# Masked global rows transposed by the DMA crossbar instead of TensorE, with mask tables for odd batches and a band mask from ScalarE

## Chip, cores and metric

One core of a Trainium2 chip. The metric is the device time of one execution in microseconds (us). Each execution is marked as fast or slow by its clock and span.

## The reference, cut to what matters

Attention over 8 batches, 8 heads, 576 positions and head size 64, followed by a gated feed-forward block on the 4608 tokens that result (model width 512, inner width 1536). A position sees its neighbours within 32 places; 8 global positions see everything and are seen by all.

```python
def _attn_ref(q, k, v, global_idx):
    ...
    mask = np.abs(pos[:, None] - pos[None, :]) <= 32
    mask = mask | is_global[:, None] | is_global[None, :]
    scores = np.where(mask, scale * (q @ k.T), -1e9)
    ...                                   # softmax, then times v

def _moe_ref(x, w_gate, w_val, w_out):
    g = x @ w_gate
    silu = g * (1.0 / (1.0 + np.exp(-g)))
    return silu * (x @ w_val) @ w_out
```

## The kernel before

The kernel splits each batch's attention into a band part and a global part. For the global part it gathers the 8 global rows of k and q, places them in a masked block `kqm` (128 partitions x 2 x 128, bf16), and transposes that to `gT`. `step_S2` multiplies `gT` with all keys, `step_SG` with all queries.

```python
def gather_mask(b, kg, qg, eng=None):
    kqms[b] = gw.tile([P, 2, 2, D], BF16, tag="kqm", name="kqm", bufs=4)
    for a, src in ((0, kg), (1, qg)):
        (eng or nc.gpsimd).tensor_tensor(
            out=kqms[b][:, a], in0=bc(src, [[0, 2], [1, D]]),
            in1=bc(mka[:, (a + b) % 2, :], [[1, 2], [0, D]]), op=ALU.mult)
...
def step_GT():
    kqm = kqms[b]
    ps = mtile([P, 2, P], BF16, "ps_g")
    for a in range(2):
        nc.tensor.transpose(out=ps[:, a, :],
            in_=kqm[:, a].rearrange("p r d -> p (r d)"), identity=ident)
    st["gT"] = gw.tile([P, 2, P], BF16, tag="gT", name="gT")
    if b % 2 == 0:
        nc.vector.tensor_copy(out=st["gT"], in_=ps)
        return
    cols = "p t (h a x) -> p (t h) a x"           # odd batches: halves swapped by the copy
    dst, src = (t.rearrange(cols, h=HP, a=2) for t in (st["gT"], ps))
    for a in range(2):
        nc.vector.tensor_copy(out=dst[:, :, a], in_=src[:, :, 1 - a])
```

The feed-forward block runs as 9 chunks of 512 tokens with 16 units each. The attention of batch b is put between the units of the chunk before its own: a table says after which unit each step goes. What SyncE and GpSimd issue (casts of k and q to bf16, crossbar transposes, loads) is placed by unit too. The code calls the point after a unit a gap. The texts below use that word, and call a unit of gate and value matmuls a gate. A casting copy (cast for short) is a DMA that turns float32 into bf16 on its way, and a DMA's landing is the moment at which it reports that it is done.

```python
        if b == 2:
            return {
                1: [L(step_GT), vb],
                2: [L(step_S2), L(step_SG)],
                ...
        return {
            1: [L(step_GT), vb],
            2: [L(step_S2), L(step_SG)] + ([L(step_P2T)] if b >= XP else []),
            ...
    cast_at, tr_at, v_at, g_at, m_at = {3: 13, 4: 26}, {2: 11, 3: 21}, {2: 8}, {2: 6}, {2: 12}
    ...
        if b > 4:
            cast_at[b] = o - 32 + 8               # o = 16 * (b - 1)
        ...
            if b % 2 == 0:
                m_at[b] = o - 16 + 13             # kqm of batches b and b + 1
```

A unit is eight gate and value matmuls or twelve output matmuls, 2.3 us on average. So the transposes come one unit before they are used. The table orders what is on one engine; GpSimd does not wait for TensorE's units, only for its own inputs and buffers (79.5 us in all until TensorE was done with a `va` buffer), and so issues the casts of k and q for batch b + 2 about when batch b's global rows are due: those of batch 6 at 142.06 and 143.76, where batch 4's rows are used at 148.52. In the head, GpSimd issues the loads of batch 1 after clearing some buffers:

```python
    def loads_b():
        kT_clear(1, nc.gpsimd)
        va_clear(1, nc.gpsimd)
        gather_mask(1, *g0)
        loaded[1] = new_qk()
        load_qk_part(1, loaded[1], 0)             # k and q of batch 1
        ...
```

The softmax here doesn't subtract the row's maximum and nothing guards it: scores larger than these inputs give would overflow.

## Time and profile before

| | before |
|---|---|
| median of 4 runs (lowest to highest) | 358.79 us (358.1 to 360.75) |
| span of the profiled run, mean clock | 356.9 us, 1.000 |
| TensorE busy | 345.9 us, 97% |
| TensorE's longest wait on a DMA after the head | none listed |
| time of one chunk in the quiet part (chunks 4 to 7) | 37.09 to 37.10 us |

The span runs from the first to the last instruction. "Busy" leaves out waits, so 97% on TensorE says that nearly all the time is TensorE's own work. The last row is my own reading of the timeline: the times at which ScalarE finishes copying the last output block of a chunk, one subtracted from the next. I use these chunk ends throughout, as they say *where* in the span a change gains or loses. The prediction below shows the profile's lines.

### The profile page before, as it was taken

To read this page: it belongs to the slowest core of one execution; us is meant where nothing else is said; L and a number is where in the kernel's file an instruction comes from. 1 tells how busy PE (TensorE), PEld (TensorE's weight loads), DVE (VectorE), ACT (ScalarE), POOL (GpSimd) and SP (SyncE) were. 2 spreads that over 40 slices of the span, in tenths; PEclk is the share of its full clock that TensorE was granted. 3 is DMA by queue.
4 is the path that set the end of the run, shared out by engine and by line. 5 is a ranking of instruction groups with operands and counts; after the bars stand their busy time and mean duration, and the time that the engine had idled before them with its cause. 6 is when DMAs were issued, how large, how long until landed. Compare 5 with 4: busy or idle time off the path is not lost.

```text
span 356.9 us, 7667 instructions
## 1 busy us (share of the span) xinstructions
PE 345.9 (97%) x3105; PEld 167.9 (47%) x3155; DVE 231.8 (65%) x469; ACT 152.9 (43%) x236; POOL 91.9 (26%) x110
## 2 busy tenths in 40 slices
PE   7889999999999999999999999999999999999996
PEld 2455445444544444444444444444444444444444
DVE  5777785289818883689368935885488637715750
ACT  4775663464324542454244522553255323323322
POOL 7974664805235113401291011000000000000000
PEclk9999999999999999999999999999999999999999
DMA  7999999999999997995899979723330230011002
GB/s 104 148 204 204 184 212 159 160 251 157 155 165 234 157 124 140 161 207 80 135 169 155 147 119 156 117 49 77 111 78 2 61 96 32 0 59 62 0 20 99
DMA packets 153540, 44.14 MB, mean 124 GB/s; under 512 B 140065, under 2 KB 148001, under 8 KB 153505
## 3 DMA queue, kind: packets, MB, share of 16 engines
q0 software_dynamic: 101216, 19.14, 65.1%
q1 hardware_dynamic: 52288, 24.51, 32.8%
q8 instruction: 24, 0.39, 0.5%
q14 instruction: 12, 0.09, 0.1%
HBM read 38.02 MB, written 16.52 MB: 153 GB/s over the span
## 4 chain that ended last, share of the span: by engine, by line
PE 90%; DVE 3%; POOL 2%; ACT 2%; issue 2%; POOLq 0%; DVEq 0%
PE pg L791 26%; PE po L852 25%; PE pv L791 25%; PE ps_s L510 3%; PE ps_av L597 3%; POOL va L102 1%; PE ps_av L588 1%; PE ps_s L444 1%; PE po L839 1%; PE ps_av L479 1%; PE ps_t L387 1%; PE ps_av L624 1%; PE pg L809 1%; PE ps_av L616 1%; PE pgv L791 0%
## 5 line engine op out<-in xcount | busy, mean ns | idle before, releaser
L791 PE MATMUL pg<-xT,wg_sb 128*128 128x512 bf16 x398 | 106.5, 380 | 1.6 <-issue 0.2
L791 PE MATMUL pv<-xT,wv_sb 128*128 128x512 bf16 x413 | 106.6, 379 | 0.2
L824 DVE SCALAR_TENSOR_TENSOR gv<-th,pg 128x512 bf16<-128x512 bf16 x107 | 73.3, 686 | 50.3 <-ACT th L822 49.5
L822 ACT ACTIVATE th<-pg 128x512 bf16<-128x512 f32 x107 | 63.9, 598 | 80.4 <-PE pg L791 78.8
L852 PE MATMUL po<-wo_sb,h 128*128 128x512 bf16 x400 | 92.7, 380 | 0.8
L828 DVE TENSOR_TENSOR h<-gv,pv 128x512 bf16<-128x512 bf16 x107 | 73.6, 688 | 11.5 <-PE pg L791 0.5
L791 PEld LDWEIGHTS <-wv_sb 128*128 128x128 bf16 x424 | 41.5, 98 | 50.0
L852 PEld LDWEIGHTS <-h 128*128 128x128 bf16 x420 | 39.4, 98 | 45.4
L791 PEld LDWEIGHTS <-wg_sb 128*128 128x128 bf16 x424 | 38.4, 98 | 43.8 <-issue 2.1
L102 POOL DMA_DIRECT2D va<-in_v_dram x40 | 35.1, 970 | 90.2 <-PE ps_av L597 79.5
L857 ACT ACTIVATE osb<-po 128x512 f32<-128x512 f32 x35 | 20.9, 597 | 81.7 <-PE po L852 67.0
L543 ACT ACTIVATE pe<-ps_s 128x1024 bf16<-128x1024 f32 (+1 forms) x39 | 36.4, 936 | 17.9 <-PE ps_s L510 17.8
L549 DVE TENSOR_TENSOR pt<-pe,band 128x1024 bf16<-128x1024 bf16 (+1 forms) x39 | 24.8, 635 | 15.3 <-ACT pe L543 14.4
L570 DVE TENSOR_TENSOR xa<-ps_av,den 128x512 bf16<-128x512 f32 (+1 forms) x40 | 25.5, 638 | 1.4
L564 DVE TENSOR_REDUCE den<-ps_av 128x8 f32<-128x16 f32 (+1 forms) x40 | 6.7, 167 | 27.5 <-PE ps_av L597 25.2
L510 PEld LDWEIGHTS <-kT 64*128 64x128 bf16 x576 | 10.7, 95 | 15.4 <-issue 15.1
L109 POOL DMA_DIRECT2D kf<-in_k_dram x6 | 13.4, 2236 | 15.9 <-issue 10.2
L109 POOL DMA_DIRECT2D qf<-in_q_dram x6 | 16.0, 2661 | 1.5 <-DMA qf<-in_q_dram 1.5
L510 PE MATMUL ps_s<-qT,kT 64*128 64x64 bf16 x576 | 15.4, 191 | 0.1
L597 PE MATMUL ps_av<-va,pt 128*64 128x66 bf16 x256 | 14.3, 197 | 0.0
L597 PE MATMUL ps_av<-vb,pt 128*64 128x66 bf16 x256 | 14.2, 197 | 0.0
L597 PEld LDWEIGHTS <-pt 128*64 128x64 bf16 x512 | 10.8, 110 | 4.2
(140 smaller groups left out, 199.9 us busy)
## 6 DMA issues: line engine op xcount, KB each, us to landing
out_dram<-osb SPq DMA_DIRECT2D x35, 256.0 KB, 2.2
vb<-va SPq DMA_DIRECT2D x14, 264.0 KB, 5.3
kf<-in_k_dram POOLq DMA_DIRECT2D x6, 576.0 KB, 16.8
qf<-in_q_dram POOLq DMA_DIRECT2D x6, 576.0 KB, 18.7
va<-in_v_dram POOLq DMA_DIRECT2D x24, 128.0 KB, 11.7
va<-in_v_dram POOLq DMA_DIRECT2D x16, 96.0 KB, 7.7
wg_sb<-in_moe_w_gate_dram POOLq DMA_DIRECT2D x3, 512.0 KB, 10.1
wv_sb<-in_moe_w_val_dram POOLq DMA_DIRECT2D x3, 512.0 KB, 12.0
```

The source lines that it names most:

```text
L102: nc.gpsimd.dma_start(out=va[lo:hi, u, :, 0:D], in_=vs[t0 + lo : t0 + hi])
L109: nc.gpsimd.dma_start(out=t, in_=src[b].rearrange("h s d -> s h d"))
L510: nc.tensor.matmul(out=ps[:, par, 64 * slot : 64 * slot + 64], lhsT=kT[r : r + 64, hp, 64 * t : 64 * t + P], rhs=qTs[b][r : r + 64, hp, 64 ...
L543: nc.scalar.activation(out=pe, in_=ps[:, :, 0 : 64 * ns].rearrange("p r (s c) -> p r s c", c=64), func=AF.Exp, scale=SCALE,)
L549: mult = lambda: nc.vector.tensor_tensor(out=pt.rearrange("p r s c -> p (r s) c"), in0=pe.rearrange("p r s c -> p (r s) c"), in1=bc(band, ...
L570: nc.vector.tensor_tensor(out=xa.rearrange("p (g h) d -> p g h d", g=g), in0=bc(ps, pst + [[1, D]]), in1=bc(den, [[4, g], [1, 4], [0, D]]) ...
L597: nc.tensor.matmul(out=ps[64 * e : 64 * e + 64, hg, hl, :], lhsT=pt[:, hl % 2, 4 * (hl // 2) + 2 * (tp % 2) + e, :], rhs=(va if e == 0 els ...
L791: nc.tensor.matmul(out=ps[:, 0:n], lhsT=w[:, cc, P * fc : P * (fc + 1)], rhs=xT[:, cc, t0 : t0 + n], start=(cc == 0), stop=(cc == NCC - 1),)
L822: nc.scalar.activation(out=th[:, 0:n], in_=pg[:, 0:n], func=AF.Tanh, scale=0.5)
L824: nc.vector.scalar_tensor_tensor(out=gv[:, 0:n], in0=th[:, 0:n], scalar=1.0, in1=pg[:, 0:n], op0=ALU.add, op1=ALU.mult,)
L828: nc.vector.tensor_tensor(out=st["h"][:, fc, 0:n], in0=gv[:, 0:n], in1=pv[:, 0:n], op=ALU.mult)
L852: nc.tensor.matmul(out=po, lhsT=st["h"][:, fc, P * ts : P * (ts + 1)], rhs=wo_sb[:, fc, :], start=(fc == 0), stop=(fc == NFC - 1),)
```

## The change

Its intent is to take work off the engine that bounds the kernel. For batches 2 to 7 the two TensorE transposes and VectorE's copy of `gT` give way to one crossbar transpose by DMA, issued by SyncE. One transpose of the whole block does not swap halves as VectorE's copy did for odd batches, so these get mask tables of their own, made by GpSimd in the head. The transposed probabilities of batch 3 go to the crossbar as well (`XP`). And the band mask, which GpSimd used to make, now comes from a square on ScalarE and a compare on VectorE, with one of the `vb` copies (`shift` 3) moved from ScalarE to GpSimd.

```diff
+    XG = 2
-    XP = 4
+    XP = 3
...
-    band = const.tile([P, 64], BF16)          # GpSimd: memset and two affine_selects
...
     def loads_b():
+        tables_odd()
...
     def squares():
+        nc.scalar.activation(out=bsq, in_=iq[:, 0:64], func=AF.Square, bias=pcol, scale=1.0)
...
     def tables_a():
+        nc.vector.tensor_scalar(out=band, in0=bsq, scalar1=R2, scalar2=None, op0=ALU.is_lt)
...
+        nc.scalar.copy(out=cnt.rearrange("p (i c) -> p i c", i=2), in_=ps_i[:, :, 0:320])
+
+    def tables_odd():
+        nc.gpsimd.memset(mg[:, 0:WIN], 0.0)
+        nc.gpsimd.memset(mg[:, WIN + S : KC], 0.0)
+        nc.gpsimd.tensor_scalar(
+            out=mg2o, in0=cnt, scalar1=thi[:, 1:2], scalar2=None, op0=ALU.is_lt
+        )
+        nc.gpsimd.tensor_tensor(out=mg2o, in0=mg2o, in1=mg, op=ALU.mult)
...
         def step_GT():
             kqm = kqms[b]
+            if b >= XG:
+                st["gT"] = gw.tile([P, 2, P], BF16, tag="gT", name="gT")
+                nc.sync.dma_start_transpose(
+                    out=st["gT"], in_=kqm.rearrange("p a r d -> p (a r d)")
+                )
+                return
...
-            if b % 2 == 0:                    # and the swapping copies of odd batches
-                nc.vector.tensor_copy(out=st["gT"], in_=ps)
-                return
...
-in0=pe, in1=mg, op=ALU.mult)
+in0=pe, in1=(mt if b % 2 else mg)[:, WIN : WIN + S], op=ALU.mult)
...
-in0=pe, in1=mg2, op=ALU.mult)
+in0=pe, in1=mg2o if b % 2 else mg2, op=ALU.mult)
...
-                L(shift, 1, act), L(step_S, 3), ...
+                L(step_S, 3), L(shift, 1, act), L(shift, 3, nc.gpsimd.tensor_copy), ...
...
         if b == 2:
-                1: [L(step_GT), vb],
+                0: [L(step_GT)],
+                1: [vb],
...                                            # b >= 3
-            1: [L(step_GT), vb],
+            -1: [L(step_GT)],
+            1: [vb],
```

The last hunk: the crossbar transpose is issued one or two units earlier than TensorE's transposes were.

More of the change, by code (lines that the diff above doesn't have):

```diff
@@ L159 @@
                    allow_small_or_imprecise_dtypes=True)
+    pcol = const.tile([P, 1], FP32)
+    nc.gpsimd.iota(pcol, pattern=[[0, 1]], base=2 * WIN, channel_multiplier=-1,
+                   allow_small_or_imprecise_dtypes=True)
     load_0("k", 1)
@@ L238 @@
     )
-    thi = const.tile([P, 1], FP32)
+    thi = const.tile([P, 2], FP32)
     nc.vector.tensor_scalar(
-        out=thi, in0=asel[:, 0:1], scalar1=1e6, scalar2=0.5, op0=ALU.mult, op1=ALU.add
+        out=thi, in0=asel, scalar1=1e6, scalar2=0.5, op0=ALU.mult, op1=ALU.add
     )
@@ L279 @@
     load_v(0)
-    band = const.tile([P, 64], BF16)
-    nc.gpsimd.memset(band, 1.0)
-    nc.gpsimd.affine_select(
-        out=band, in_=band, compare_op=ALU.is_ge, fill=0.0,
-        base=0, pattern=[[-1, 64]], channel_multiplier=1,
-    )
-    nc.gpsimd.affine_select(
-        out=band, in_=band, compare_op=ALU.is_ge, fill=0.0,
-        base=2 * WIN, pattern=[[1, 64]], channel_multiplier=-1,
-    )
     load_wgv(0)
@@ L307, in loads_b @@
             )
-    mg = const.tile([P, S], BF16)
+    mg = const.tile([P, KC], BF16)
     mg2 = const.tile([P, KC], BF16)
+    mg2o = const.tile([P, KC], BF16)
+    cnt = const.tile([P, KC], BF16)
     m1 = const.tile([P, KC], BF16)
+    band = const.tile([P, 64], BF16)
+    bsq = const.tile([P, 64], FP32)
     def squares():
+        nc.scalar.activation(out=bsq, in_=iq[:, 0:64], func=AF.Square, bias=pcol, scale=1.0)
         nc.scalar.activation(out=iq, in_=iq, func=AF.Square, bias=ngcol, scale=1.0)
@@ L326, in tables_a @@
         nc.vector.tensor_scalar(
-            out=mg, in0=iq[:, WIN : WIN + S], scalar1=sgn[:, 0:1], scalar2=thr[:, 0:1],
+            out=mg[:, WIN : WIN + S], in0=iq[:, WIN : WIN + S], scalar1=sgn[:, 0:1], scalar2=thr[:, 0:1],
             op0=ALU.mult, op1=ALU.is_gt,
@@ L338, in tables_b @@
         nc.vector.scalar_tensor_tensor(
-            out=mg2.rearrange("p (i c) -> p i c", i=2), in0=ps_i[:, :, 0:320], scalar=thi,
+            out=mg2.rearrange("p (i c) -> p i c", i=2), in0=ps_i[:, :, 0:320], scalar=thi[:, 0:1],
             in1=mt.rearrange("p (i c) -> p i c", i=2), op0=ALU.is_lt, op1=ALU.mult,
         )
+        nc.scalar.copy(out=cnt.rearrange("p (i c) -> p i c", i=2), in_=ps_i[:, :, 0:320])
[6 more added lines that the diff above has]
+        nc.gpsimd.tensor_tensor(out=mg2o, in0=mg2o, in1=mg, op=ALU.mult)
     def warm(*widths):
@@ L409, in step_GT @@
             st["gT"] = gw.tile([P, 2, P], BF16, tag="gT", name="gT")
-            if b % 2 == 0:
-                nc.vector.tensor_copy(out=st["gT"], in_=ps)
-                return
-            cols = "p t (h a x) -> p (t h) a x"
-            dst, src = (t.rearrange(cols, h=HP, a=2) for t in (st["gT"], ps))
-            for a in range(2):
-                nc.vector.tensor_copy(out=dst[:, :, a], in_=src[:, :, 1 - a])
+            nc.vector.tensor_copy(out=st["gT"], in_=ps)
         def step_SG():
@@ L433, in step_SG @@
             st["pg"] = bp.tile([P, S], BF16, tag="pg", name="pg")
-            mult = lambda: nc.vector.tensor_tensor(out=st["pg"], in0=pe, in1=mg, op=ALU.mult)
+            mult = lambda: nc.vector.tensor_tensor(out=st["pg"], in0=pe, in1=(mt if b % 2 else mg)[:, WIN : WIN + S], op=ALU.mult)
             if b == 0:
@@ L455, in step_S2 @@
             st["p2"] = work.tile([P, KC], BF16, tag="p2", name="p2")
-            mult = lambda: nc.vector.tensor_tensor(out=st["p2"], in0=pe, in1=mg2, op=ALU.mult)
+            mult = lambda: nc.vector.tensor_tensor(out=st["p2"], in0=pe, in1=mg2o if b % 2 else mg2, op=ALU.mult)
             if b == 0:
@@ L719, in attention @@
                 L(step_S, 1), L(step_P2T), M("e*"), M("p*", 1), L(shift, 0, dve),
-                L(shift, 1, act), L(step_S, 3), L(warm, 512, 512), L(step_AV2), M("p*", 5),
+                L(step_S, 3), L(shift, 1, act), L(shift, 3, nc.gpsimd.tensor_copy), L(warm, 512, 512), L(step_AV2), M("p*", 5),
                 L(shift, 2, act), L(warm, 512, 512, 512),
                 L(step_AV, 0), M("xa*", 0), L(warm, 512, 256), L(step_AV, 1), M("p*", 3),
-                L(step_X, 0), L(shift, 3, act), L(warm, 256), L(step_AV, 2), M("xa*", 1),
+                L(step_X, 0), L(warm, 256), L(step_AV, 2), M("xa*", 1),
                 L(warm, 512, 512), M("xa*", 2), L(step_X, 1), L(step_AV, 3), M("xa*", 3),
```

## The prediction

No term of its main sum is among them: 4.2 + 1.5 + 3.5 = 9.2 us lost and 0.6 gained, net 8.6, and with it 368 us. GpSimd's new work in the head was put at about 4 us, which gives the 23.5 at which batch 1's loads would be issued. The clock (rival 2) was to bring the time up to 371 us. In the "quiet stretch" at 182.3 a cast had been issued too, 0.5 us before the store (181.78); at 145.3 the two casts had been issued 3.2 and 1.5 us before.

> **What bounds the kernel now.** I read the page first, then the list of waits, then the timeline around one batch's global rows, then the DMA issues of narrow stretches.
>
> From the page:
>
> ```profile
> PE 345.9 (97%) x3105; PEld 167.9 (47%) x3155; DVE 231.8 (65%) x469; ACT 152.9 (43%) x236; POOL 91.9 (26%) x110
> PEclk9999999999999999999999999999999999999999
> DMA  7999999999999997995899979723330230011002
> PE 90%; DVE 3%; POOL 2%; ACT 2%; issue 2%; POOLq 0%; DVEq 0%
> ```
>
> TensorE bounds it: 97% busy, 90% of the chain that ended last, full clock. Four 512-column matmuls take 0.86 us in the chain, 0.216 us each. [...]a microsecond of waiting anywhere after the head is a microsecond at the end. The DMA row matters next: the engines are nearly full for the first 60% of the span (batches 0 to 4) and lightly loaded after that. No wait of TensorE on a DMA stands in the list of waits after the first loads. From the list (engine, line, releaser: total us, times, longest):
>
> ```profile
> DVE pt L549 <- ACT pe L543: 14.4, 26, 3.1
> PEld L444 <- DVE gT L411: 2.4, 4, 1.2
> PEld L444 <- DVE gT L416: 1.3, 3, 0.4
> PE ps_s L444 <- DVE gT L411: 1.0, 1, 1.0
> DVE pt L549 <- POOL band L286: 0.9, 1, 0.9
> ```
>
> L444 is the first use of gT, the transposed global rows. It waits for VectorE's copy, but most of that is weight-load time that overlaps matmuls: the matmuls themselves waited 1.0 us once, for batch 0. The last line is the band mask that GpSimd makes late in the head.
>
> The timeline of batch 4, around its global rows (start, duration):
>
> ```profile
> 145.27 0.53 SPq L859 DMA_DIRECT2D out_dram<-osb  x1
> 145.72 1.03 PE L791 MATMUL pv<-xT,wv_sb 128*128 128x512 bf16 x4
> 146.07 0.47 SPq L129 DMA_DIRECT2D vb<-va  x1
> 146.58 0.28 PE L405 MATMUL ps_g<-ident,kqm 128*128 128x128 bf16 x2
> 146.70 1.03 PE L791 MATMUL pg<-xT,wg_sb 128*128 128x512 bf16 x4
> 147.56 1.03 PE L791 MATMUL pv<-xT,wv_sb 128*128 128x512 bf16 x4
> 148.52 0.46 PE L444 MATMUL ps_s<-kT,gT 128*32 128x320 bf16 x8
> ```
>
> The two transposes cost 146.70 - 146.58 = 0.12 us of TensorE. The rows are needed at 148.52. The built program shows where the crossbar transpose goes in SyncE's queue: behind the output store issued at 145.27 and ahead of the vb copy issued at 146.07. So its neighbours tell when it could land. The DMA issues of the stretches 145.2 to 145.3 and 146.0 to 146.1 (last number: median us to landing):
>
> ```profile
> out_dram<-osb SPq DMA_DIRECT2D x1, 256.0 KB, 6.1
> vb<-va SPq DMA_DIRECT2D x1, 264.0 KB, 7.8
> ```
>
> The store lands at 145.27 + 6.1 = 151.4 and vb at 153.9, both well after 148.52. This reading decides the prediction.
>
> [...]SyncE's transfers land in issue order, 2.2 us after issue for a store in a quiet stretch (182.3) but 6.1 us at 145.3, while GpSimd's casting copies run.[...] The change leaves three gates, about 5 us.[...]
>
> **The change, part by part.**
>
> Removed from TensorE: two transposes in each of batches 2 to 7, 6 x 0.11 = 0.7 us; the gap of about 0.1 us ahead of L444 where VectorE's copy is late, up to 0.5 us; the five transposes of batch 3's masked probabilities, now also on the crossbar, 0.29 us (115.68 to 115.97). Together 1.3 to 1.5 us. VectorE loses about 2.3 us of copies (six of 0.216 and three of 0.284 for batches 2 to 7, and a little in batch 1) and ScalarE a copy of 0.69 us. Both have slack, so nothing comes of it.
>
> Head: the band mask no longer comes from GpSimd (0.74 us of work, and VectorE's wait of 0.94 us until 13.51). The new square of 64 columns on ScalarE (estimate 0.26 us, between 0.20 us for one column and 0.83 us for 640) fits in its 3.0 us wait for ngcol; VectorE's compare fits in its 0.38 us wait before mt. The count copy (estimate 0.70 us, as p2e of the same width) delays exponentials whose results waited for the band anyway. So batch 0's gT copy can start about 0.8 us earlier and the head shortens by up to 0.8 us.
>
> [...]The loads of batch 1, issued at 19.3, would be issued at about 23.5. The weight loads before them keep the engines full until about 28 (GpSimd waits for the last wv_sb until 27.97), so they should land as before, at 29 to 34.
>
> Added on the critical path: waits for gT. Six crossbar transposes must land within 3 to 5 us of being issued.
> - Batch 2: SyncE issues four stores from 67.65, after it was held by the kT and qT transposes. The stores take a median of 7.1 us, the last is issued at 69.3 and lands near 78.0 (its trace landing is 8.7 us after issue). gT comes behind it, near 78.0; L444 began at 73.77. Loss 4.2 us. This time is set by the DMA engines, so the head's gain is swallowed here.
> - Batch 3: stores of that stretch take 6.3 us, the third is issued at 106.58, hence gT near 112.7 against 111.14. Loss 1.5 us.
> - Batch 4: gT near 152.0 against 148.52. Loss 3.5 us.
> - Batches 5 to 7: quiet DMA; crossbar transposes of similar size land in 2.3 to 2.4 us. Issued at about 183.0, 220.1 and 257.6, gT lands at 185.4, 222.5, 260.0 against 185.61, 222.71, 259.80: even, or 0.2 us gained or lost each.
>
> Sum: 4.2 + 1.5 + 3.5 = 9.2 us lost; about 0.6 us gained (0.3 for batch 3's transposes, 0.3 in batches 5 to 7). Net +8.6, or 368 us.
>
> **The rivals.**
> 1. *gT lands in time everywhere.* kqm is ready long before (about 61 us for batches 2 and 3), and a transpose of 64 KB is small. Then the sum is -0.8 (head) - 1.4 = about 357.2 us. For it: the kernel before is scheduled closely and never waits for a DMA (batch 4's p2t, 8.1 us to landing, arrives just in time), so someone may have placed this with care too. Against it[...]landings of 6 to 9 us on both sides of it.
> 2. *The waits cost the clock too.* [...]up to 371 us.
> 3. *The head gets worse.* If GpSimd's new work takes 7 us rather than 4, the loads of batch 1 start late, the engines idle, and batch 1's first transposes (32.6, with about 1.7 us of slack) wait: 1 to 2 us more, which passes on through batch 2's casts. For it: GpSimd's spans stretch[...] (a 128x128 multiply took 0.39 us, but up to 2.0 us once). Against it: some 4 us of queue ahead.
> 4. *The waits shrink each other.* A wait in batch 2 lets the DMA engines catch up, so batches 3 and 4 wait less: about 362 to 364 us. Against it: GpSimd's casts are released by TensorE's progress there, so they shift too.
>
> **Range and chances.** I give the late landing (368, or 362 to 371 with rivals 2 to 4) about 65%, the timely one (357) about 35%. The middle of that mixture is about 366 us. Slower by over 2% means above 366.6, which most but not all of the first case reaches: 0.45. Faster by over 2% would need 352.3, for which no part of the sum is large enough: 0.02. Range 357 to 371.5.
>
> **What would show each step.** Right: new waits of TensorE at ps_s<-kT,gT on the DMA gT<-kqm, 4 us in batch 2, 1 to 2 in batch 3, 3 to 4 in batch 4 and next to nothing in batches 5 to 7, with gT 5 to 9 us from issue to landing in the first three and 2.4 in the rest; a unit of 16 steps in the quiet part (37.09 us, 217.32 to 254.41) shorter by 0.1 to 0.2 us; VectorE's wait on band gone. Wrong: no such waits, gT landing within 4 us under load, and a time near 357; or a wait of batch 1's transposes on k_bf or q_bf, which would be rival 3; or a PEclk digit below 9, rival 2.

## The result, and the profile after

| | before | after |
|---|---|---|
| median of 4 runs (lowest to highest) | 358.79 us (358.1 to 360.75) | 381.46 us (380.26 to 383.14) |
| span and mean clock of the profiled run | 356.9 us, 1.000 | 379.4 us, 0.978 |

The ratio is 1.0626 with a 95% interval of 1.0564 to 1.0687: slower. (Ratios are the mean time of one kernel's fast runs over the mean of the other's fast runs of the same rounds, so not quite the ratio of the medians quoted.) The output was correct. 381.46 us is outside the predicted range of 357 to 371.5.

From the page of the kernel after (busy us and share of the span; then the clock and DMA rows of the 40 slices; then the chain that ended last):

```profile
PE 349.1 (92%) x3088; PEld 168.0 (44%) x3138; DVE 230.3 (61%) x460; ACT 152.0 (40%) x235; POOL 96.2 (25%) x114
...
PEclk9999999969999999969998999999999999999999
DMA  8999999999999938995499959880350051002002
...
PE 59%; DMA 16%; POOL 11%; issue 9%; SPq 2%; DVE 2%; ACT 0%; POOLq 0%
```

TensorE has fewer instructions than before (3088 against 3105) and yet is busy for 3.2 us longer, because three stretches, in slices 9, 18 and 22, ran at a lower clock. The chain that was 90% TensorE is now 59%, with DMA at 16%. TensorE's waits on DMAs after the head, which the kernel before did not have (line and releaser: total us, times, longest):

```profile
PE ps_s L457 <- DMA gT<-kqm: 18.6, 5, 6.8
...
PE ps_av L610 <- DMA vb<-va: 1.4, 1, 1.4
```

L457 is the first use of `gT` (L444 before). Batch by batch, in TensorE's timeline of the kernel after (start, duration, and in brackets how long TensorE had stood and for what):

```profile
79.45 0.72 PE L457 MATMUL ps_s<-kT,gT 128*32 128x320 bf16 x8 [5.92 <-DMA gT<-kqm]
...
121.20 0.46 PE L457 MATMUL ps_s<-kT,gT 128*32 128x320 bf16 x8 [2.87 <-DMA gT<-kqm]
...
205.61 0.72 PE L457 MATMUL ps_s<-kT,gT 128*32 128x320 bf16 x8 [2.09 <-DMA gT<-kqm]
...
282.19 0.46 PE L457 MATMUL ps_s<-kT,gT 128*32 128x320 bf16 x8 [0.94 <-DMA gT<-kqm]
```

Batches 2, 3, 5 and 7; batch 6 did not wait. After two of these the eight matmuls took 0.72 us where they take 0.46 otherwise. Batch 4 with what SyncE did before it, from the timeline of the kernel after:

```profile
156.58 0.33 SPq L874 DMA_DIRECT2D out_dram<-osb  x1
157.02 1.93 SPq L418 DMA_TRANSPOSE gT<-kqm  x1
...
157.22 1.03 PE L806 MATMUL pv<-xT,wv_sb 128*128 128x512 bf16 x4
...
165.04 0.72 PE L457 MATMUL ps_s<-kT,gT 128*32 128x320 bf16 x8 [6.79 <-DMA gT<-kqm]
```

TensorE was through with its last value matmul at 157.22 + 1.03 = 158.25 and had nothing to do until 165.04. Its `gT` had been asked for only 1.2 us before 158.25. From there to the landing it took, in the DMA issues of a narrow stretch of the kernel after around batch 4's (last number: us to landing):

```profile
gT<-kqm SPq DMA_TRANSPOSE x1, 8.0
```

The same view gives 7.8, 6.9, 8.0, 4.7, 2.3 and 2.3 us for batches 2 to 7. The transfer is the same 64 KB each time.

**The clock.** The view of chosen windows of the kernel after (start and end; length, then the busy time of TensorE with its count of instructions, weight loads, VectorE, ScalarE, GpSimd; then granted clock, DMA share and GB/s). In this trace the clock was at half speed from 75.88 to 82.70, from 161.20 to 168.03 and from 205.58 to 208.99, so for 6.82, 6.83 and 3.41 us, and at full speed in between. The windows have the length of the shortest of these; the last two end and begin where the clock fell, and the first two, where it did not, begin 12 and 13 such lengths after 75.88:

```profile
116.84:120.25 3.41, 1.49 (x7) 0.49 (x5) 2.31 (x4) 0.60 (x1) 0.00 (x0) 1.00 1.99 200
120.25:123.66 3.41, 2.41 (x24) 1.22 (x26) 1.07 (x3) 1.80 (x3) 0.00 (x0) 1.00 1.70 231
...
202.17:205.58 3.41, 1.34 (x7) 0.39 (x4) 2.17 (x4) 0.60 (x1) 3.41 (x5) 1.00 1.19 91
...
205.58:208.99 3.41, 3.38 (x22) 1.32 (x23) 0.95 (x2) 1.57 (x3) 0.24 (x1) 0.51 1.92 248
```

At batch 5 TensorE was busy for 1.34 us of one window and the next ran at 0.51, with 3.38 us of matmul time in it. At batch 3 it was busy for 1.49 us and the next ran at full clock. The two stretches at batches 2 and 4, 75.88 to 82.70 and 161.20 to 168.03, have 3.25 and 2.99 us of matmul time in them. At half speed the next four matmuls of 512 columns began after 1.68 us (166.18 to 167.86), at full speed after 0.87 (168.83 to 169.70). So if half of the busy time at half speed is lost, the loss is an estimated 1.6, 1.5 and 1.7 us for batches 2, 4 and 5, together 4.8 us.

**The sum.** How far the kernel after trails the kernel before at the end of each chunk, and what the rows above make of it (us; a batch's wait falls in the chunk of the same number, counted from 1; each transposed batch saves 0.12, batch 3's crossbar probabilities 0.28, and both savings come from the kernels below):

| chunk | behind at its end | added in it | wait | clock | savings | worked out |
|---|---|---|---|---|---|---|
| 1 | -0.19 | -0.19 | | | | |
| 2 | 7.23 | 7.42 | 5.92 | 1.62 | -0.12 | 7.42 |
| 3 | 9.78 | 2.55 | 2.87 | | -0.40 | 2.47 |
| 4 | 17.95 | 8.17 | 6.79 | 1.50 | -0.12 | 8.17 |
| 5 | 21.60 | 3.65 | 2.09 | 1.69 | -0.12 | 3.66 |
| 6 | 21.50 | -0.10 | 0 | | -0.12 | -0.12 |
| 7 | 22.39 | 0.89 | 0.94 | | -0.12 | 0.82 |
| 8 and 9 | 22.40 | 0.01 | | | | |

The profile accounts for the loss: 18.6 us of waits, 4.8 us of clock, 1.0 us saved, against a difference of the spans of 22.5. What is left to test is why `gT` was late, whether the waits alone explain it, and what the rest of the change is worth.

**The head.** GpSimd's timeline, before:

```profile
19.29 0.76 POOL L80 DMA_DIRECT2D k_bf<-in_k_dram  x1
```

and after:

```profile
18.39 2.11 POOL L351 TENSOR_SCALAR mg2o<-cnt,thi 128x640 bf16<-128x640 bf16 x1
20.59 1.61 POOL L354 TENSOR_TENSOR mg2o<-mg2o,mg 128x640 bf16<-128x640 bf16 x1
...
24.87 0.78 POOL L81 DMA_DIRECT2D k_bf<-in_k_dram  x1
```

The new compare and multiply took 3.7 us, and the first load of batch 1 was issued 5.6 us later. By the end of chunk 1 the kernel after is nevertheless 0.19 us ahead. This profiled run had an early head: batch 1's first use of `gT` began 0.90 us sooner than before (41.63 against 42.53), and the wait of 1.4 us on `vb` used that up. The other changed kernels came to that point within 0.4 us of the kernel before.

### The profile page after: what moved, and what is told of

It is laid out like the page before. It is cut to its first block, busy times and chain, and to the rows that moved or that the text cites. A ratio compares the mean times of both kernels' runs of the same rounds, so it can differ in the third digit from the quotient of the medians.

```text
span 379.4 us, 7641 instructions
## 1 busy us (share of the span) xinstructions
PE 349.1 (92%) x3088; PEld 168.0 (44%) x3138; DVE 230.3 (61%) x460; ACT 152.0 (40%) x235; POOL 96.2 (25%) x114
## 4 chain that ended last, share of the span: by engine, by line
PE 59%; DMA 16%; POOL 11%; issue 9%; SPq 2%; DVE 2%; ACT 0%; POOLq 0%
PE pg L806 18%; PE po L867 17%; PE pv L806 17%; DMA gT<-kqm 6%; DMA va<-in_v_dram 5%; POOL va L103 3%; DMA wv_sb<-in_moe_w_val_dram 3%; PE ps_s L523 2%; PE ps_av L610 2%; DMA kg<-in_k_dram,gofs 2%; POOL qf L110 2%; SPq L689 1%; POOL kf L110 1%; PE ps_av L601 1%; PE ps_s L457 1%
## 5 line engine op out<-in xcount | busy, mean ns | idle before, releaser
L806 PE MATMUL pg<-xT,wg_sb 128*128 128x512 bf16 x394 | 109.0, 387 | 1.6
L806 PE MATMUL pv<-xT,wv_sb 128*128 128x512 bf16 x417 | 107.9, 381 | 0.1
L457 PE MATMUL ps_s<-kT,gT 128*32 128x320 bf16 x64 | 4.5, 363 | 18.6 <-DMA gT<-kqm 18.6
L464 ACT ACTIVATE p2e<-ps_s 128x640 bf16<-128x640 f32 x8 | 5.6, 704 | 24.5 <-PE ps_s L457 24.5
## 6 DMA issues: line engine op xcount, KB each, us to landing
kf<-in_k_dram POOLq DMA_DIRECT2D x6, 576.0 KB, 13.8
va<-in_v_dram POOLq DMA_DIRECT2D x24, 128.0 KB, 7.5
```

Source lines behind the costliest of these rows:

```text
L806: nc.tensor.matmul(out=ps[:, 0:n], lhsT=w[:, cc, P * fc : P * (fc + 1)], rhs=xT[:, cc, t0 : t0 + n], start=(cc == 0), stop=(cc == NCC - 1),)
```

## The experiments

The theory: `gT` is asked for too late for a loaded DMA system, TensorE stands, and the stand costs clock as well. The rivals: the new tables and late loads in the head cause the loss; or the wait alone costs and the clock follows from something else; or the output store ahead of it in SyncE's queue is what delays `gT`.

All kernels gave correct output. Medians of 4 runs unless noted; the kernel before ran beside them at 359.02 to 359.05.

| kernel | median us (lowest to highest) | ratio to before, 95% | clock of the profiled run |
|---|---|---|---|
| e1_gt_on_pe | 359.8 (359.32 to 360.68) | 1.0019, 0.9995 to 1.0043 | 0.999 |
| e2_early | 360.23 (359.56 to 360.33) | 1.0022, 1.0003 to 1.0041 | 1.000 |
| e3_fill | 377.25 (377.04 to 379.38) | 1.0519, 1.0482 to 1.0556 | 1.000 |
| e4_head | 381.91 (378.73 to 384.81), one run marked slow | 1.0659, 1.0599 to 1.0718 | 0.982 |
| e5_early_head | 360.88 (360.46 to 361.36) | 1.0051, 1.003 to 1.0071 | 1.000 |
| e6_cast_later | 380.48 (378.94 to 381.27) | 1.0578, 1.0549 to 1.0607 | 0.973 |
| e7_before_store | 374.4 (370.17 to 375.2) | 1.0383, 1.032 to 1.0447 | 0.982 |
| e8_xg3_early_head | 359.19 (358.96 to 360.36), 6 runs | 1.0007, 0.9989 to 1.0025 | 1.000 |

### e1_gt_on_pe: the change without the crossbar rows

```diff
-    XG = 2
+    XG = 8
-                0: [L(step_GT)],
-                1: [vb],
+                1: [L(step_GT), vb],
...
-            -1: [L(step_GT)],
-            1: [vb],
+            1: [L(step_GT), vb],
```

> The changed kernel with the global rows of batches 2 to 7 transposed by TensorE again, at their old places; the odd tables, the band, the shift on GpSimd and batch 3's crossbar p2t stay. Theory (the lost time is the late gT and the clock that falls after it): the five waits on gT, 18.6 us, and the halved clock, about 4.9 us, both go; 357 to 359.5 us. Rival (the rest of the change, head or odd tables, costs several us of its own): 362 us or more.

Measured: 359.8 us, ratio 1.0019, 0.3 us over the range expected. All but about 0.7 us of the loss is in the crossbar rows; tables, band mask, moved copy and batch 3's probabilities together leave the time the same within noise. TensorE's list of waits of this kernel has no `gT` from a DMA but has a new one in batch 2:

```profile
PE ps_sg L435 <- DMA qT<-qf: 1.0, 1, 1.0
```

It is ahead of the kernel before by 0.23 us at the end of chunk 1, behind by 0.95 at the end of chunk 2, and by 0.67 to 0.73 from chunk 3 on. So the later loads of the head cost about 1 us in batch 2, where the queries come late (in e8, with the loads early again, that wait is 0.32 us), and batch 3's probabilities on the crossbar give back 0.28.

### e2_early: the crossbar rows issued five units earlier

```diff
-                0: [L(step_GT)],
+                -5: [L(step_GT)],
...
-            -1: [L(step_GT)],
+            -6: [L(step_GT)],
...
-{2: 11, 3: 21}, {2: 8}, {2: 6}, {2: 12}
+{2: 10, 3: 21}, {2: 8}, {2: 6}, {2: 10}
...
-                m_at[b] = o - 16 + 13
+                m_at[b] = o - 16 + 9
```

The last two edits only make `kqm` ready that early (and issue batch 2's transposes of k and q one unit earlier).

> The crossbar transposes stay, but SyncE issues them earlier: for batches 3 to 7 five gaps earlier, between the xT transposes of the batch before; for batch 2 right behind kT and qT, ahead of three or four stores. Theory (gT is late only because of where it stands in SyncE's queue): waits on gT gone in batches 3 to 7, at most 2 us in batch 2, where it lands just behind qT; clock 1.0; 357 to 361 us. Rival (crossbar transposes of these rows are slow or disturb the other transfers wherever they stand): waits of several us stay or move to other tiles, above 365 us.

Measured: 360.23 us, ratio 1.0022, clock 1.0. The same transfers still took 6.2, 7.9 and 6.3 us to land in batches 2 to 4, and 2.3 to 4.0 after that, but nobody waited for them except batch 2. TensorE's waits on DMAs in this kernel:

```profile
PE ps_s L457 <- DMA gT<-kqm: 1.9, 1, 1.9
...
PE ps_av L610 <- DMA vb<-va: 0.7, 1, 0.7
PE ps_av L492 <- DMA p2t<-p: 0.6, 1, 0.6
```

This is the main proof: only the point of issue changed in substance, and 21 us came back. It also measures what the crossbar saves. A quiet chunk took 36.98 us against 37.10 before, 0.12 us less per batch, just what two transposes cost on TensorE. Batch 2's 1.9 us stays: `gT` there follows the transposes of k and q, of which the second held SyncE from 63.58 for 5.59 us, and so was issued at 69.22, 4.4 us before it was needed.

### e3_fill: TensorE kept busy while it waits

```diff
-                2: [L(step_S2), L(step_SG)],
+                2: [L(warm, *[512] * 23), L(step_S2), L(step_SG)],
...
-            2: [L(step_S2), ...
+            2: ([L(warm, *[512] * {3: 10, 4: 27, 5: 7}[b])] if b < 6 else []) + [L(step_S2), ...
```

67 matmuls whose result nobody uses, 0.216 us each, in the place of most of the waits.

> The changed kernel with matmuls that nothing reads put before the first use of gT in batches 2 to 5 (23, 10, 27, 7 of 512 columns, 0.216 us each), about as long as the waits there. gT comes as late as before. Theory (the waits also halve the clock, which costs 4.9 us of the 22): waits on gT below 1 us each, clock 1.0 throughout, 375 to 378 us. Rival (the clock costs nothing measurable beside the waits): 380 to 383 us.

Measured: 377.25 us; the clock row and the wait of this kernel:

```profile
PEclk9999999999999999999999999999999999999999
```

```profile
PE ps_s L457 <- DMA gT<-kqm: 4.3, 4, 1.3
```

Three of the waits left are 1.2 to 1.3 us, a little over the 1 us expected. Fill and waits are 67 x 0.216 + 4.3 = 18.8 us, as much as the 18.6 us of waits in the kernel after. With the same lateness but little idle TensorE, the clock of the profiled run never dropped (of the other runs, the one of 379.38 us had 0.995), and the ratio fell from 1.0626 to 1.0519, that is by 0.0107 x 359 = 3.8 us. This confirms the clock as a cost of its own; the 4.8 us estimated from the windows is somewhat more than what the time shows. From the end of chunk 1 on, where the different heads of the two profiled runs no longer count, this kernel loses 18.05 us and the kernel after 22.59, 4.5 us more.

### e4_head: the head's loads before the new tables

```diff
     def loads_b():
-        tables_odd()
...
         load_wgv(2)
+        tables_odd()
...
-L(shift, 1, act), L(shift, 3, nc.gpsimd.tensor_copy), ...
+L(shift, 1, act), ...
-                L(step_X, 0), L(warm, 256), ...
+                L(step_X, 0), L(shift, 3, act), L(warm, 256), ...
```

> The changed kernel with shift 3 back on ScalarE and GpSimd's odd tables made after batch 1's loads are issued. Theory (GpSimd's new work in the head delays batch 1's loads by 1.2 us on landing, which shows as the 1.4 us wait on vb and as 1 to 2 us of batch 2's 5.9 us): loads issued at 19 to 20 us, no wait on vb, batch 2's wait 4 to 5 us, 378 to 379.5 us. Rival (the loads are bound by the DMA engines and land at the same time): no change, 381 us.

Measured: 381.91 us with one run marked slow and a wide spread, where 378 to 379.5 was expected; in time it says nothing beyond that most of the loss is not in the head. The ratio of 1.0659 comes out only with the run marked slow counted in; its three fast runs, averaging 380.85 us, make it about 1.060. The spread goes with the clock: the runs of 378.73 and 380.35 us had a mean clock of 0.982, those of 383.48 and 384.81 us (the one marked slow) 0.969. So how much of a run falls at half speed differs between runs of one kernel; in the kernel after, too, it ranged from 0.969 to 0.978. In its profile, batch 1's loads were issued at 18.45 instead of 24.87, the wait on `vb` was gone, batch 2's k arrived in bf16 at 56.2 instead of 57.9, and batch 2 waited 5.17 us for `gT` instead of 5.92. All waits on `gT` summed to 16.5 us.

### e5_early_head: e2 and e4 together

The edits are those of e2 and e4.

> e2_early and e4_head together: gT issued early, batch 1's loads issued before GpSimd's odd tables, shift 3 on ScalarE. Theory (in batch 2 the rows can land no sooner than qT, which the DMA engines set, and the loads' delay moves qT by 1.2 us): wait on gT in batch 2 falls from 1.9 to about 1 us, the wait on vb is gone, 358.8 to 360 us against e2's 360.2. Rival (the head's order of loads makes no difference to the end): 360.2 us and the same waits.

Measured: 360.88 us, ratio 1.0051: no better than e2, and over what I had hoped. Two of its four runs had a clock of 0.995 and took 361.3 us; the two at 0.999 to 1.0 took 360.5. The `vb` wait is gone and batch 2's wait for `gT` is 1.3 instead of 1.9 us, but TensorE's timeline of this kernel has another in its place:

```profile
107.65 1.04 PE L806 MATMUL pg<-xT,wg_sb 128*128 128x512 bf16 x4 [0.52 <-DMA xT<-xa]
```

and the wait of 0.6 us on `p2t` of batch 4 stays. At the end of chunk 2 it is 1.20 us behind the kernel before (e2: 1.72), at the end of chunk 4 2.04 (e2: 1.88). What TensorE saved by chunk 2, transfers took back by chunk 4.

### e6_cast_later: batch 6's casting copies moved away from batch 4's rows

```diff
-            cast_at[b] = o - 32 + 8
+            cast_at[b] = 67 if b == 6 else o - 32 + 8
```

The casts of k and q for batch 6, in GpSimd's timeline of the kernel after:

```profile
151.84 2.23 POOL L110 DMA_DIRECT2D kf<-in_k_dram  x1
153.53 2.76 POOL L110 DMA_DIRECT2D qf<-in_q_dram  x1
```

That is 5.2 and 3.5 us before batch 4's `gT`; here GpSimd issues them at 193.51 and 195.22, 3.8 and 2.1 us before batch 5's.

> The changed kernel with one thing moved: GpSimd's casting copies of batch 6, which ran while batch 4's gT was under way, are put in its queue behind batch 6's v loads, so they run some 45 us later, beside those of batch 7, while batch 5's gT is under way. Theory (gT lands late where casting copies run at the same time): batch 4's gT lands 2.3 to 4 us after issue instead of 8.0, its wait falls from 6.8 to 1 to 2.5 us and the clock no longer halves there; batch 5's wait stays or grows, from 2.1 to 2 to 5 us; 374 to 380 us. Rival (gT is late because of the store and the transposes ahead of it in SyncE's queue, whatever GpSimd does): batch 4's wait stays at 5 to 7 us, 381 us.

Measured: 380.48 us, 0.5 us over the range expected and as near to the rival's 381; the waits decide between them. Batch 4, and TensorE at batch 5, in the timeline of this kernel:

```profile
160.12 0.33 SPq L874 DMA_DIRECT2D out_dram<-osb  x1
160.56 1.19 SPq L418 DMA_TRANSPOSE gT<-kqm  x1
...
162.90 0.46 PE L457 MATMUL ps_s<-kT,gT 128*32 128x320 bf16 x8 [0.98 <-DMA gT<-kqm]
...
204.95 0.73 PE L457 MATMUL ps_s<-kT,gT 128*32 128x320 bf16 x8 [5.00 <-DMA gT<-kqm]
```

Its `gT` landed 2.3 us after issue instead of 8.0, with the same store ahead of it in the queue, and TensorE waited 0.98 instead of 6.79 us. Batch 5's `gT`, now behind these casts as well, took 7.6 us instead of 4.7, and TensorE waited 5.00 instead of 2.09. The lateness went where the casts went. The total hardly changed because the loss moved from batch 4 to batch 5, and because the clock halved after batch 3's wait, 3.21 us here: TensorE was busy for 0.91 us from 117.8 to 121.2, and from there to 128.0 the clock was 0.50.

### e7_before_store: the crossbar rows ahead of the output store

```diff
-                0: [L(step_GT)],
+                -2: [L(step_GT)],
...
-            -1: [L(step_GT)],
+            -2: [L(step_GT)],
```

The theory of this run, whose wording is cut from the recorded text, was that each place in SyncE's queue counts.

> The changed kernel with gT issued one step earlier in all six batches: ahead of the last of the stores of that stretch instead of behind it. Theory[...]: each wait shorter by 0.5 to 1.5 us, batch 7's gone, 375 to 379 us; still a wait of 4 us or more in batches 2 and 4, since the transposes of xT stand ahead of it there. Rival (only the casting copies count): waits as before, 381 us.

Measured: 374.4 us, ratio 1.0383, a little below the range expected. One place in the queue is worth 0.0243 x 359 = 8.7 us, less than half the loss. TensorE's waits on DMAs in this kernel:

```profile
PE ps_s L457 <- DMA gT<-kqm: 10.4, 3, 5.3
...
PE ps_av L492 <- DMA p2t<-p: 1.5, 1, 1.5
```

Batches 2, 3 and 4 wait 5.32, 0.64 and 4.42 us and batches 5 to 7 not at all; the clock halves after batches 2 and 4 (0.50 from 77.6 to 84.4 and from 159.5 to 166.3). From issue to landing `gT` took 7.5 and 7.3 us in batches 2 and 3, hardly different from the 7.8 and 6.9 of the kernel after; batch 3 gained by being issued 6.7 instead of 4.1 us before it was needed. In batch 4 it took 6.0 us instead of 8.0. So there the store ahead is worth 2 us of the landing and the casts, by e6, nearly 6; in the other batches the two are not told apart. Once `gT` goes first, batch 5's `p2t` comes late instead.

### e8_xg3_early_head: the best I could make of it

e5, with batch 2 left on TensorE.

```diff
-    XG = 2
+    XG = 3
-                0: [L(step_GT)],
-                1: [vb],
+                1: [L(step_GT), vb],
```

> The best of it: e5 with batch 2's rows on TensorE again, so nothing of batch 2 waits for a crossbar transpose of its own. Theory: no wait on gT, at most 0.5 us on qT in batch 2, some 0.6 us on batch 4's p2t as in e2; 0.12 us gained in each of batches 3 to 7 and 0.28 us by batch 3's p2t on the crossbar: 357.8 to 359 us, 0 to 0.4% faster than the kernel before. Rival (the gain is eaten by another wait): 359 to 360 us.

Measured in 5 rounds: 359.19 us, ratio 1.0007, 0.9989 to 1.0025: the same as the kernel before, and in the rival's range. TensorE is busy for 345.1 us, 0.8 less than before, and it is 0.14 us behind at the end of the last chunk. Three short waits on DMAs are left after the head, one of them in its timeline at batch 2:

```profile
74.31 0.43 PE L435 MATMUL ps_sg<-qT,gT 128*32 128x288 bf16 x8 [0.32 <-DMA qT<-qf]
```

the others of 0.32 us on `xT` at 106.50 and of 0.16 us on `p2t` of batch 5. No version that I ran beats the kernel before.

## Why the prediction was wrong

The direction and the mechanism were right: new waits at `ps_s<-kT,gT` on the DMA, worst where casting copies run, and a clock that answers. The sizes were not, and the number (366.0) came out 15.5 us short. Point by point:

- **gT in batches 2 to 4: "4.2 + 1.5 + 3.5 = 9.2".** The waits were 5.92, 2.87 and 6.79, together 15.6. This is the step that failed. I took the landing of a new transfer from the landing of its neighbours in the trace before, as if adding it moved nothing and it landed about when the store ahead of it did. In the kernel after it landed 0.87, 1.19 and 1.63 us behind that store, where I had 0, -0.2 and 0.6 (106.58 + 6.3 is 112.9 and not 112.7). Issuing it also took its own time: 1.18 to 1.93 us of SyncE, against 0.33 to 0.53 for the store beside it, and the transposes of `xT` show about 1.2 us in the trace before already. For batch 3 this covers what was missing. In batch 2, besides, k in bf16 landed some 1.9 us later, its transposes were issued at 57.93 instead of 56.04 and the last store landed at 78.54 instead of 77.99, while the rows were needed 0.23 us sooner; with the 0.87 that makes 1.65 of the 1.7 us missing. In batch 4, SyncE had fallen behind: the store ahead of `gT` was issued 1.67 us before the rows were needed (156.58 against 158.25), where the trace before has it 3.25 us ahead (145.27 against 148.52). 1.6 of the 3.3 us missing are that; the rest is the landing, which I put 6.7 us after the store's issue and which took 8.4.
- **Batches 5 to 7: "even, or 0.2 us gained or lost".** They lost 2.09, 0 and 0.94. I called the stretch quiet; in batch 5 the casts of batch 7 were issued at 199.72 and 201.46, around `gT` at 200.85, and it took 4.7 us instead of 2.3. In batch 7 the landing was 2.3 as foreseen, but SyncE came to it late: it issued `gT` 1.4 us before it was needed and not 2.2, after a transpose of `xT` that had held it for 2.48 us.
- **Rival 2, the clock.** I gave it, up to 371, as a side case, with a cost per wait that no trace had shown. Three halvings came, of an estimated 1.6, 1.5 and 1.7 us; I had not put the clock into the sum, nor the number of waits that would reach it. e3 shows by the time that about 3.8 us go to it.
- **The sum.** The median before, 358.79, and the net 8.6 make 367.4 and not 368. From there to 381.5 are 14.1 us: 6.4 more waiting in batches 2 to 4, 3.0 in batches 5 and 7 and an estimated 4.8 of clock, less 0.4 of savings beyond the 0.6 entered, together 13.8.
- **Rival 3, the head.** Partly real. GpSimd's new work delayed batch 1's loads by 5.6 us, not about 4, which was my estimate: the compare took 2.11 us and the multiply 1.61. No transpose of batch 1 waited noticeably, so the sign that I named did not show; a wait of 1.4 us on `vb` did, and by the end of chunk 1 nothing of it was left; that run's early head had made up for it. The price came in batch 2, 1 us by e1, through the casts.
- **Rival 4, waits that shrink each other.** Wrong: batch 4 waited longest of all.
- **Rival 1 and the chances.** e2 shows that rival 1 would have been right in batches 3 to 7 for a kernel that issues early; this one did not. Giving it 35% pulled the number from 368 to 366 (a mean with these weights would be 364) and the lower end of the range to 357. The upper end of 371.5 allowed for the clock but for no error in the 9.2.
- **What held.** The savings: 0.12 us per transposed batch and 0.28 for batch 3's probabilities, against 0.11 and 0.29. VectorE's wait on the band mask is gone. "The head's gain is swallowed" in batch 2: e1 shows it, with transfers setting the pace. The head's gain itself, "up to 0.8 us", was smaller: batch 0's first use of `gT` moved from 14.45 to 14.09 to 14.16 in the eight experiments, 0.3 us. (The profiled run of the kernel after has 13.34; no other run repeats that, and why is not settled.) A wait of 0.3 to 0.8 us for ScalarE's new count copy took part of it, which I had thought hidden.

Left open: a single `xT` transpose usually holds SyncE for 1.2 us but now and then 2.1 to 2.5 us (2.39 at 151.13 in the kernel after), which is part of why SyncE fell behind; no run tells why. And e4 was too noisy to say what the head's order does to the time. A version with no casts at all near the rows was not tried.

## What to carry to other kernels

Before a transfer takes over work from the engine that bounds the kernel, look at how long such a transfer takes at that place in the program, with the load around it and with its own issue added, and issue it at least that early; here up to 8 us were needed to replace 0.12 us of TensorE work, and the source had been ready. Beside a wait of TensorE, allow for the clock that may halve after it: here waits of 2.09, 5.92 and 6.79 us cost an estimated 1.5 to 1.7 us more each, one of 2.87 us nothing. And where the DMA engines are about as full as TensorE (90% or more in most of the first 24 of 40 slices of the kernel before), small savings on TensorE can be taken back by the next transfer, as in e5 and e8.
